# Expert weights in eight larger loads, landed in buffers of later work, with their splits spread over steps 5 to 12

## The chip, the cores and the metric

The kernel runs on one core of a Trainium2 chip. The metric is the device time of one execution in microseconds (us). The engines are TensorE (PE, with its weight loads as PEld), VectorE (DVE), ScalarE (ACT), GpSimd (POOL) and SyncE (SP), which issues all plain DMAs of this kernel; the indirect DMAs are issued by POOL.

## The reference

Attention with eight heads over eight batches: 512 local queries look at a window of 32 keys to either side and at 32 global keys, 32 global queries look at everything. Its output, 576 rows of 512 per batch, goes through a layer in which the 128 rows of highest gate score get an expert's output added.

```
s_l  = concat(scale * q_l @ k_g.T, where(|i-j| <= 32, scale * q_l @ k_l.T, -1e9))
out_l = softmax(s_l) @ concat(v_g, v_l);  out_g = softmax(scale * q_g @ k_all.T) @ v_all
x = concat(out_g, out_l) as [B, 576, 512]
scores = x @ w_gate
top = argpartition(-scores[b], 128)[:128]
out[b, top] = x[b, top] + sigmoid(scores[b, top]) * (relu(x[b, top] @ w1) @ w2)
```

## The kernel before

The attention of one batch is six pieces of work, in the order `ORDER`: local tiles L0 and L1 (128 queries, all heads), the two global halves G0 and G1, then L2 and L3. With eight batches there are 48 steps; step `i` of the loop is piece `i % 6` of batch `i // 6`. The program order on each engine is written out by hand and pipelined: in step `i` PE runs the attend matmuls of piece `i-1` (L260 for a local, L349 for a global piece), the scores of piece `i+1` (L201, L314) and the transposes of piece `i` (L238, L341). ACT then copies the transposed probabilities to SBUF (`pt`, L247 or L244) and takes the exponential of piece `i+1` (L228, L328). DVE divides the output (`x`, L280), takes the maxima (`mxl`, L215; `mx`, L318) and the gate score of each output tile (L297, with the gate row `wgb`). Each engine executes its own list in order, so whatever waits holds all that is behind it.

The expert's weights are `w1` and `w2`, 2 MiB each in fp32. Each of 16 blocks of 128x512 is split into a high part (a cast on ACT, L153) and the rest (a subtraction on POOL, L154). `load_w` loads one block of 256 KB into `ws`, a ring of three buffers (`wst`), and `split` makes the two parts. The main loop issues two loads in each of the steps 1 to 8 and, at the end of a step from step 2 on, splits all blocks loaded so far but the last. The split stands in ACT's list behind the exponential of that step, so ACT's next copy `pt` is behind it.

A batch's K, Q and V come through `load(b)` (for batch 1 issued in step 1) and `load_v(b, t)`, V in a ring of four buffers of 1040 KB. `load_rest` brings the gate row, the index constants and the masks of the ranking in step 0. Stores of finished tiles are issued by `run_stores` at the head of a step, ahead of that step's loads. `load_xg` reads a batch's global rows back from the output.

A batch's ranking is a generator, `chain`, started in step 6b+7. For batch 0 the score rows are spread in step 9 (`spread`), ranked in steps 9, 10 and 11 (`rank`, pairs of DVE instructions L395 and L397), the one-hot matrix is made in step 11 (L407), the rows are gathered in step 12 (an indirect DMA of POOL, L427, into `xe`), and the expert's work on them begins in step 14 with `expand` (transposes L448), which fills `xTh` and `xTl`; `ffn1_row`, `ffn1_turn` and `ffn1_pair` fill `hTh` and `hTl`. Which step gets how much of that work is set by `GROUPS`, `DUE` and `run_fill` in steps, not in time. L106 to L125 are the loads of the start, L287 the stores of `x`, L365 those of the global rows, L369 `load_xg`.

## Time and profile before

| what | value |
|---|---|
| time, median of 3 runs | 361.35 us (360.27 to 363.27) |
| profiled execution, its own time | 363.92 us |
| its span in the trace | 361.9 us |
| PE busy / PEld busy | 283.1 us (78%) / 224.4 us (62%) |
| DVE, ACT, POOL busy | 203.7 us (56%), 166.9 us (46%), 37.7 us (10%) |
| bytes moved by DMA | 75.89 MB, mean 210 GB/s |
| share of "DMA ws<-in_w_dram" in the chain that ended last | 9% |

The shares are means over a start that waits for loads, a long middle and an end of expert work alone. Each stretch is read by itself, by what its engines wait for.

### The profile page before, as it was taken

The numbers are of one execution on the slowest core, as the hardware profiler recorded it, in microseconds if no ns is written. First come the engines' busy times: TensorE is split into PE (matmuls) and PEld (weight loads), VectorE is DVE, ScalarE is ACT, GpSimd is POOL, SyncE is SP. The second block draws the span as 40 slices with busy tenths as digits, with TensorE's granted clock in tenths as the row PEclk, the third lists the DMA queues.
The fourth block names the chain that finished last, engine by engine and source line by source line (L and its number), as shares of the span: only waits on it lengthen the run. The fifth ranks groups of instructions, "written<-read, shape, count | busy, mean of one in ns | idle before, by whom it ended". The sixth has DMA issues, their size and how long they took to land.

```text
span 361.9 us, 14027 instructions
## 1 busy us (share of the span) xinstructions
PE 283.1 (78%) x6200; PEld 224.4 (62%) x6200; DVE 203.7 (56%) x561; ACT 166.9 (46%) x483; POOL 37.7 (10%) x38
## 2 busy tenths in 40 slices
PE   5373855367759869978787799998768999599994
PEld 2342743246537746755566788876648887389882
DVE  1142363329844748695776665787756656639122
ACT  1253755257644745673476336354763361032020
POOL 1002444141100000100200001101000011110211
PEclk9699696869989989998999999999999999779998
DMA  7996579944992696189569912995691011100100
GB/s 215 405 412 243 183 265 378 372 137 146 362 369 75 239 415 264 42 307 423 215 210 345 361 38 66 385 361 200 211 340 57 34 43 60 59 29 2 58 29 29
DMA packets 22652, 75.89 MB, mean 210 GB/s; under 512 B 4672, under 2 KB 7616, under 8 KB 17600
## 3 DMA queue, kind: packets, MB, share of 16 engines
q1 hardware_dynamic: 21312, 70.81, 52.7%
q0 software_dynamic: 1280, 4.20, 3.4%
q8 instruction: 48, 0.79, 0.9%
q14 instruction: 12, 0.10, 0.1%
HBM read 63.98 MB, written 11.01 MB: 207 GB/s over the span
## 4 chain that ended last, share of the span: by engine, by line
PE 41%; issue 17%; DMA 17%; ACT 11%; DVE 7%; SPq 3%; POOL 3%; POOLq 0%; ACTq 0%
DMA ws<-in_w_dram 9%; ACT p_t L228 5%; PE m_ps L509 5%; PE s_ps L260 5%; PE s_ps L201 5%; PE s_ps L238 5%; PE m_ps L525 4%; DMA wgb<-in_wg_dram 4%; DMA xe<-out_dram,ix 4%; PE s_ps L314 3%; ACT pt L247 3%; PE s_ps L349 3%; PE s_ps L341 2%; PE s_ps L509 2%; ACT pt L244 2%
## 5 line engine op out<-in xcount | busy, mean ns | idle before, releaser
L228 ACT ACTIVATE p_t<-s_ps,nb 128x128 f32<-128x128 f32 x256 | 69.7, 384 | 1.0
L247 ACT COPY pt<-s_ps 128x512 f32<-128x512 f32 x64 | 34.4, 589 | 61.3 <-PE s_ps L238 61.3
L260 PE MATMUL s_ps<-v_t,pt 128*32 128x65 f32 x2048 | 39.5, 229 | 27.0 <-ACT pt L247 22.5
L260 PEld LDWEIGHTS s_ps<-v_t,pt 128*32 128x32 f32 x2048 | 33.4, 115 | 36.0 <-ACT pt L247 27.8
L215 DVE TENSOR_REDUCE mxl<-s_ps 128x8 f32<-128x1024 f32 x32 | 39.0, 1220 | 29.3 <-PE s_ps L201 29.3
L201 PE MATMUL s_ps<-k_t,q_t 64*32 64x128 f32 x2048 | 40.5, 286 | 10.1 <-DMA k_t<-in_kT_dram 6.4
L238 PE MATMUL s_ps<-cs,p_t 128*128 128x128 f32 x256 | 37.3, 291 | 4.8 <-issue 2.7
L201 PEld LDWEIGHTS s_ps<-k_t,q_t 64*32 64x32 f32 x2048 | 30.7, 110 | 13.9 <-issue 11.5
L238 PEld LDWEIGHTS s_ps<-cs,p_t 128*128 128x128 f32 x256 | 29.5, 148 | 11.2 <-issue 5.5
L349 PE MATMUL s_ps<-v_t,pt 128*32 128x65 f32 x768 | 16.1, 239 | 17.2 <-ACT pt L244 17.2
L244 ACT COPY pt<-s_ps 128x768 f32<-128x768 f32 x16 | 12.8, 799 | 30.9 <-PE s_ps L341 30.9
L349 PEld LDWEIGHTS s_ps<-v_t,pt 128*32 128x32 f32 x768 | 13.3, 121 | 21.4 <-ACT pt L244 19.5
L274 DVE TENSOR_SCALAR den<-s_ps 128x8 f32<-128x8 f32 x32 | 5.2, 164 | 37.3 <-PE s_ps L260 36.0
L427 POOL DMA_INDIRECT xe<-out_dram,ix x8 | 7.9, 985 | 169.3 <-DVE junk L395 133.7
L395 DVE SCALAR_TENSOR_TENSOR junk<-r,sc,side_w 128x128 bf16<-128x128 f32 (+4 forms) x40 | 24.4, 611 | 0.9 <-ACT r L383 0.2
L297 DVE CUSTOM_DVE_ANT_0 junk<-x,wgb 128x512 bf16<-128x512 f32 x32 | 23.3, 728 | 0.3 <-DMA wgb<-in_wg_dram 0.2
L280 DVE TENSOR_TENSOR x<-s_ps,rec 128x512 f32<-128x512 f32 x32 | 22.1, 691 | 1.2 <-DVE rec L276 0.2
L509 PE MATMUL m_ps<-xTh,w1h 128*128 128x256 f32 x76 | 19.8, 291 | 2.8 <-DVE hTl L512 2.8
L397 DVE SCALAR_TENSOR_TENSOR junk<-r,sc,side_w 128x544 bf16<-128x544 f32 (+4 forms) x40 | 20.6, 516 | 2.1 <-ACT nb L222 0.2
L314 PE MATMUL s_ps<-k_t,qg_t 64*32 64x512 f32 (+1 forms) x256 | 20.1, 429 | 0.0
L509 PE MATMUL m_ps<-xTh,w1l 128*128 128x256 f32 x76 | 19.0, 283 | 0.0
L532 POOL DMA_INDIRECT out_dram<-xe,ix x8 | 8.1, 1011 | 87.8 <-DVE xe L530 63.3
(111 smaller groups left out, 474.9 us busy)
## 6 DMA issues: line engine op xcount, KB each, us to landing
v_t<-in_vw_dram SPq DMA_DIRECT2D x32, 1040.0 KB
k_t<-in_kT_dram SPq DMA_DIRECT2D x7, 1664.0 KB
out_dram<-x SPq DMA_DIRECT2D x32, 256.0 KB
q_t<-in_qT_dram SPq DMA_DIRECT2D x15, 512.0 KB
ws<-in_w_dram SPq DMA_DIRECT2D x16, 256.0 KB
k_t<-in_kT_dram SPq DMA_DIRECT2D x1, 1152.0 KB
q_t<-in_qT_dram SPq DMA_DIRECT2D x2, 256.0 KB
k_t<-in_kT_dram SPq DMA_DIRECT2D x1, 512.0 KB
```

The lines of the kernel that those rows point to most:

```text
L201: nc.tensor.matmul(out=s_ps[32 * j:32 * j + 32, hp, P * pr:P * pr + P], lhsT=q_t[t // 2][rows, pr, 32 * (c % 8):32 * (c % 8) + 32], rhs=wi ...
L215: nc.vector.tensor_reduce(out=mx, in_=s_ps.rearrange("p a (r k) -> p (a r) k", k=P), axis=AX.X, op=ALU.max)
L228: nc.scalar.activation(out=p_t[:, hp, cc], in_=s_ps[:, hp, cc], func=AF.Exp, scale=0.125, bias=nb[:, k:k + 1])
L238: nc.tensor.transpose(s_ps[:, hp, cc], p_t[:, hp, cc], ident)
L247: nc.scalar.copy(out=pt[:, hp], in_=s_ps[:, hp])
L260: nc.tensor.matmul(out=s_ps[32 * j:32 * j + 32, hp, VD * pr:VD * pr + VD], lhsT=pt[:, hp, x0:x0 + 32], rhs=v_t[:, j, NPAIR * hp + pr, :], ...
L280: nc.vector.tensor_tensor(out=xt[b, t].rearrange("p r a d -> p a r d"), in0=o_ps[:, :, :, 0:D], in1=rec.broadcast_to([P, 2, NPAIR, D]), op ...
L297: nc.vector.tensor_tensor_reduce(out=junk[:n, 0:DM], in0=xf, in1=wgb[:n], op0=ALU.mult, op1=ALU.add, scale=1.0, scalar=0.0, accum_out=dst,)
L314: nc.tensor.matmul(out=o_, lhsT=qg_t[rows, pr, :], rhs=r_, start=True, stop=True)
L349: nc.tensor.matmul(out=og[32 * h:32 * h + 32, :], lhsT=ptg[:, P * i + 32 * h:P * i + 32 * h + 32], rhs=vts[b, c // 4][:, c % 4, NPAIR * (h ...
L395: nc.vector.scalar_tensor_tensor(out=junk[:n, 0:hi], in0=r[:n, 0:hi], scalar=s, in1=side_w[:n, P + SL - lo:P + SL - lo + hi], op0=ALU.is_g ...
L509: nc.tensor.matmul(out=h_ps, lhsT=a[:, kc, ms], rhs=xT[x_][:, kc, :], start=(i == 0), stop=(i == len(prods) - 1))
```

## The change

The eight loads of `load_w` are now pieces of different sizes. Pieces 0 and 1 are 1 MiB of `w1` each and land in tiles named `hTh` and `hTl`, pieces 2 to 5 are 256 KB blocks of `w2` in the four `xe` buffers, pieces 6 and 7 are 512 KB of `w2` in `xTh` and `xTl`. These buffers are used by the expert's work only from step 12 on. `LOADW` says in which step each piece is issued, `SPLITS` how many of the 16 blocks are split in which step. The ring `ws` shrinks to two buffers. The gate row moves from `load_rest` into `load(0)`; all four V tiles of batch 0 are issued ahead of the loop; `load_rest` moves to step 1 behind `load(1)`; in every step the stores and `load_xg` come behind the loads.

```
-RESTL, LATE, WFIRST = 0, 4, 1
+RESTL, LATE = 1, 4
+LOADW = {2: (0,), 3: (1,), 6: (2, 3), 7: (4, 5), 8: (6, 7)}
+SPLITS = {5: 1, 6: 2, 7: 2, 8: 4, 9: 2, 10: 1, 11: 2, 12: 2}
...
-    wst = ctx.enter_context(tc.tile_pool(name="wst", bufs=3))
+    wst = ctx.enter_context(tc.tile_pool(name="wst", bufs=2))
...
             load_v(0, 0)
+            nc.sync.dma_start(out=wgb, in_=wg)
             nc.sync.dma_start(out=q_t[0][:, :, P:], in_=qT[b, 0, :, :, P:])
...
+    def load_w(k):
+        if k < 2:
+            s = moe.tile([P, 2, FF], FP32, name=("hTh", "hTl")[k])
+            nc.sync.dma_start(out=s, in_=w1[:, 2 * k:2 * k + 2])
+            for n in range(4):
+                raw[4 * k + n] = s[:, n // 2, 512 * (n % 2):512 * (n % 2) + 512]
+        elif k < 6:
+            s = moe.tile([P, DM], FP32, name="xe", bufs=4)
+            nc.sync.dma_start(out=s, in_=w2[:, k - 2])
+            raw[6 + k] = s
+        else:
+            s = moe.tile([P, 2, DM], FP32, name=("xTh", "xTl")[k - 6])
+            m = 2 * k - 8
+            nc.sync.dma_start(out=s, in_=w2[:, m:m + 2])
+            raw[8 + m], raw[9 + m] = s[:, 0], s[:, 1]
...
     load(0)
-    load_v(0, 1)
-    wl = []
+    for t in range(1, NT):
+        load_v(0, t)
+    wl = list(range(2 * KC + MC))
...
         if i < nstep:
-            run_stores()
-            if s == 0:
+            if s == 0 and b > 0:
                 load_v(b, 2)
-            if i == RESTL:
-                load_rest()
             if s == 1:
-                load_v(b, 3)
+                if b > 0:
+                    load_v(b, 3)
                 if b + 1 < B:
                     load(b + 1)
             if s == 5:
-                load_xg(b)
                 if b + 1 < B:
                     load_v(b + 1, 0)
                     load_v(b + 1, 1)
-            if WFIRST <= i < WFIRST + 8:
-                wl.append(load_w(2 * (i - WFIRST)))
-                wl.append(load_w(2 * (i - WFIRST) + 1))
+                load_xg(b)
+            if i == RESTL:
+                load_rest()
+            for k in LOADW.get(i, ()):
+                load_w(k)
+            run_stores()
...
-        if i > WFIRST:
-            while wl[-2:-1] if WFIRST <= i < WFIRST + 8 else wl:
-                split(*wl.pop(0))
+        for _ in range(SPLITS.get(i, 0)):
+            split(wl.pop(0))
```

Three places in the order of the instructions follow. The first is ACT's list in steps 1 to 4 of the kernel before. L247 and L244 are the copies `pt` of a local and a global piece, L328 and L228 exponentials, L153 the casts of the splits.

```order
8 L247 COPY pt<-s_ps 128x512 x2
9 L328 ACTIVATE pg<-s_ps,nbg 128x64
10 L328 ACTIVATE pg<-s_ps,nbg 128x5x96
11 L244 COPY pt<-s_ps 128x768
12 L328 ACTIVATE pg<-s_ps,nbg 128x64
13 L328 ACTIVATE pg<-s_ps,nbg 128x5x96
14 L153 CAST w1h<-ws 128x512 x3
15 L244 COPY pt<-s_ps 128x768
16 L222 ACTIVATE nb<-mxl 128x8
17 L228 ACTIVATE p_t<-s_ps,nb 128x128 x8
18 L153 CAST w1h<-ws 128x512 x2
```

In the change the same stretch of ACT's list has no cast (all its line numbers behind `load_w` are 17 higher).

```order
8 L264 COPY pt<-s_ps 128x512 x2
9 L345 ACTIVATE pg<-s_ps,nbg 128x64
10 L345 ACTIVATE pg<-s_ps,nbg 128x5x96
11 L261 COPY pt<-s_ps 128x768
12 L345 ACTIVATE pg<-s_ps,nbg 128x64
13 L345 ACTIVATE pg<-s_ps,nbg 128x5x96
14 L261 COPY pt<-s_ps 128x768
15 L239 ACTIVATE nb<-mxl 128x8
16 L245 ACTIVATE p_t<-s_ps,nb 128x128 x8
```

The three casts that stood between an exponential and the copy of step 3 are gone from there. The second place is ACT's list in steps 8 and 9 of the change, where most casts stand now (L400 and L403 copy the score rows that `spread` turned).

```order
34 L345 ACTIVATE pg<-s_ps,nbg 128x64
35 L345 ACTIVATE pg<-s_ps,nbg 128x5x96
36 L180 CAST w1h<-hTl 128x512 x3
37 L180 CAST w2h<-xe 128x512
38 L400 COPY r<-m_ps 128x512
39 L403 COPY r<-m_ps 128x32
40 L261 COPY pt<-s_ps 128x768
41 L239 ACTIVATE nb<-mxl 128x8
42 L245 ACTIVATE p_t<-s_ps,nb 128x128 x8
43 L180 CAST w2h<-xe 128x512 x2
44 L264 COPY pt<-s_ps 128x512 x2
```

Before, two casts stood at the first of these two places and one at the second; the block at the first place grew to four, and from here on two, one, two and two casts stand at the end of the steps 9 to 12. The third place is SP's list behind the first loads. Before:

```order
10 L125 DMA v_t<-in_vw_dram 128x2080 x2
11 L632 DMA wgb<-in_wg_dram 128x512
12 L633 DMA cs<-in_const_dram 128x133
13 L634 DMA side_w<-in_edge_dram 128x128
14 L635 DMA side_w<-in_edge_dram 128x128
15 L125 DMA v_t<-in_vw_dram 128x2080
16 L115 DMA q_t<-in_qT_dram 128x1024
17 L116 DMA k_t<-in_kT_dram 128x3328
18 L117 DMA q_t<-in_qT_dram 128x1024
19 L118 DMA qg_t<-in_qgT_dram 128x128
20 L160 DMA ws<-in_w_dram 128x512 x2
21 L287 DMA out_dram<-x_317 128x512
```

In the change, the same loads and what follows them:

```order
12 L118 DMA q_t<-in_qT_dram 128x1024
13 L119 DMA k_t<-in_kT_dram 128x3328
14 L120 DMA q_t<-in_qT_dram 128x1024
15 L121 DMA qg_t<-in_qgT_dram 128x128
16 L649 DMA cs<-in_const_dram 128x133
17 L650 DMA side_w<-in_edge_dram 128x128
18 L651 DMA side_w<-in_edge_dram 128x128
19 L160 DMA hTh<-in_w_dram 128x2048
20 L304 DMA out_dram<-x_313 128x512
21 L160 DMA hTl<-in_w_dram 128x2048
22 L304 DMA out_dram<-x_380 128x512
```

The weights still stand behind all loads of batches 0 and 1, but as two transfers of 1 MiB that wait for no buffer.

## Rows read from the trace of the kernel before

**Rows 1.** The waits of the whole span: who waited for whom, us in total, times, longest.

```profile
ACT w2h L153 <- DMA ws<-in_w_dram: 14.2, 3, 8.5
ACT w1h L153 <- DMA ws<-in_w_dram: 6.8, 3, 4.8
PE s_ps L201 <- DMA k_t<-in_kT_dram: 6.4, 1, 6.4
```

**Rows 2.** The timeline, ACT's part: start, duration, engine, line, operation, count, and in brackets the idle time before it and what ended it. Two copies `pt` without a split ahead of them, then the three longest waits of casts.

```profile
22.93 1.07 ACT L247 COPY pt<-s_ps 128x512 f32<-128x512 f32 x2 [1.18 <-PE s_ps L238]
27.13 0.80 ACT L244 COPY pt<-s_ps 128x768 f32<-128x768 f32 x1 [2.36 <-PE s_ps L341]
...
33.49 1.27 ACT L153 CAST w1h<-ws 128x512 fp32r<-128x512 f32 x2 [4.79 <-DMA ws<-in_w_dram]
...
55.89 0.62 ACT L153 CAST w2h<-ws 128x512 fp32r<-128x512 f32 x1 [5.33 <-DMA ws<-in_w_dram]
...
73.85 0.62 ACT L153 CAST w2h<-ws 128x512 fp32r<-128x512 f32 x1 [8.53 <-DMA ws<-in_w_dram]
```

**Rows 3.** The timeline, PE's part: the attend matmuls that open steps 1, 2, 3, 4, 7, 9, 10, 11, 12 and 13 (L260 local, L349 global), and the transposes of step 3 (L341).

```profile
19.48 1.14 PE L260 MATMUL s_ps<-v_t,pt 128*32 128x65 f32 x64 [1.16 <-ACT pt L247]
...
24.05 1.13 PE L260 MATMUL s_ps<-v_t,pt 128*32 128x65 f32 x64 [1.16 <-ACT pt L247]
...
27.98 0.89 PE L349 MATMUL s_ps<-v_t,pt 128*32 128x65 f32 x48 [0.72 <-ACT pt L244]
...
29.89 0.88 PE L341 MATMUL s_ps<-cs,pg 128*128 128x128 f32 x6
...
36.76 1.53 PE L349 MATMUL s_ps<-v_t,pt 128*32 128x65 f32 x48 [5.78 <-ACT pt L244]
...
57.53 1.96 PE L260 MATMUL s_ps<-v_t,pt 128*32 128x65 f32 x64 [6.34 <-ACT pt L247]
...
75.22 1.53 PE L349 MATMUL s_ps<-v_t,pt 128*32 128x65 f32 x48 [7.91 <-ACT pt L244]
...
81.49 0.89 PE L349 MATMUL s_ps<-v_t,pt 128*32 128x65 f32 x48 [0.72 <-ACT pt L244]
...
86.06 1.14 PE L260 MATMUL s_ps<-v_t,pt 128*32 128x65 f32 x64 [0.94 <-ACT pt L247]
...
90.64 1.15 PE L260 MATMUL s_ps<-v_t,pt 128*32 128x65 f32 x64 [0.94 <-ACT pt L247]
...
96.47 1.17 PE L260 MATMUL s_ps<-v_t,pt 128*32 128x65 f32 x64 [0.98 <-ACT pt L247]
```

**Rows 4.** SP's timeline: two pairs of the weight loads with the time that SP spent at them.

```profile
25.94 9.86 SPq L160 DMA_DIRECT2D ws<-in_w_dram  x2
...
66.70 9.47 SPq L163 DMA_DIRECT2D ws<-in_w_dram  x2
```

**Rows 5.** Stretches of the span: from:to, length, busy us (and instructions) of PE, PEld, DVE, ACT, POOL, then the granted TensorE clock as a share of full speed, the DMA engines' busy share, and GB/s.

```profile
0.00:8.50 8.50, 5.22 (x76) 2.15 (x76) 0.88 (x3) 1.49 (x2) 1.19 (x6) 1.00 0.70 211
8.50:19.50 11.00, 3.69 (x76) 3.10 (x76) 1.90 (x2) 3.53 (x12) 0.00 (x0) 0.69 1.03 399
19.50:28.70 9.20, 7.19 (x224) 5.11 (x224) 5.00 (x14) 5.62 (x16) 0.00 (x0) 1.00 1.03 408
28.70:35.90 7.20, 2.28 (x85) 1.70 (x73) 1.83 (x4) 1.75 (x4) 1.71 (x2) 0.94 0.59 223
...
51.20:57.50 6.30, 0.00 (x0) 0.00 (x0) 1.26 (x3) 1.61 (x4) 1.62 (x2) 0.84 1.02 360
57.50:67.30 9.80, 8.60 (x176) 5.79 (x176) 5.31 (x14) 5.74 (x16) 4.11 (x4) 0.75 1.00 380
...
75.20:98.80 23.60, 18.38 (x607) 14.63 (x607) 17.10 (x46) 16.11 (x50) 5.50 (x5) 0.91 0.60 209
98.80:288.00 189.20, 161.59 (x4011) 128.40 (x4012) 126.30 (x353) 100.33 (x295) 6.83 (x7) 0.97 0.64 238
```

**Rows 6.** A DMA issue of the page's part 6: what it moves, times, size.

```profile
wgb<-in_wg_dram SPq DMA_DIRECT2D x1, 256.0 KB
```

**Rows 7.** DVE beside POOL: POOL's subtraction of one split and a ranking instruction of DVE of 128x256 that began 0.32 us after it; then the same instruction a batch later, with no work on POOL.

```profile
84.34 1.27 POOL L154 TENSOR_TENSOR w2l<-ws,w2h 128x512 fp32r<-128x512 f32 x1 [5.32 <-ACT w2h L153]
84.66 1.23 DVE L395 SCALAR_TENSOR_TENSOR junk<-r,sc,side_w 128x256 bf16<-128x256 f32 x1
...
118.75 0.48 DVE L395 SCALAR_TENSOR_TENSOR junk<-r,sc,side_w 128x256 bf16<-128x256 f32 x1
```

**Rows 8.** The line L297 (gate scores), its 32 instructions on `x`: min/median/max duration in ns, first and last start.

```profile
L297 DVE CUSTOM_DVE_ANT_0 junk<-x,wgb x32: 679/682/1219, 22.9 to 307.0; 128x512 bf16<-128x512 f32 x32
```

**Rows 9.** DVE's timeline at the turn from step 11 to step 12: the one-hot matrix, then the maxima that the next exponential needs.

```profile
93.17 0.82 DVE L407 TENSOR_TENSOR oh<-slot,rank 128x640 f16<-128x640 f16 x1
...
94.95 1.22 DVE L215 TENSOR_REDUCE mxl<-s_ps 128x8 f32<-128x1024 f32 x1
```

**Rows 10.** The timeline at the first gather: the exponential of step 12 on ACT, the gather on POOL, and the PE work that waits for it.

```profile
96.56 2.18 ACT L228 ACTIVATE p_t<-s_ps,nb 128x128 f32<-128x128 f32 x8
...
97.13 1.12 POOL L427 DMA_INDIRECT xe<-out_dram,ix  x1 [11.52 <-DVE ix L425]
...
106.65 1.08 PE L448 MATMUL m_ps<-cs,xe 128*128 128x128 f32 x4 [2.61 <-DMA xe<-out_dram,ix]
```

**Rows 11.** The last line of the view of the tile `xe`: the time from issue to landing of its DMAs.

```profile
DMA to landing us min/median/max: 2.7/3.3/9.5
```

More of the change, by code (lines that the diff above doesn't have):

```diff
@@ L150, with split @@
     slot16 = cst.tile([P, NST * P], FP16, name="slot16")
-    def split(hi, lo, src):
+    raw = {}
+    def load_w(k):
[13 more added lines that the diff above has]
+            raw[8 + m], raw[9 + m] = s[:, 0], s[:, 1]
+    def split(k):
+        if k < 2 * KC:
+            c = (slice(None), k // 2, slice(512 * (k % 2), 512 * (k % 2) + 512))
+            hi, lo = w1h[c], w1l[c]
+        else:
+            hi, lo = w2h[:, k - 2 * KC], w2l[:, k - 2 * KC]
+        src = raw.pop(k)
         nc.scalar.copy(out=hi, in_=src)
         nc.gpsimd.tensor_tensor(out=lo, in0=src, in1=hi.bitcast(FP32), op=ALU.subtract)
-    def load_w(k):
-        s = wst.tile([P, 512], FP32, name="ws")
-        if k < 2 * KC:
-            kc, f = k // 2, slice(512 * (k % 2), 512 * (k % 2) + 512)
-            nc.sync.dma_start(out=s, in_=w1[:, kc, f])
-            return w1h[:, kc, f], w1l[:, kc, f], s
-        k -= 2 * KC
-        nc.sync.dma_start(out=s, in_=w2[:, k])
-        return w2h[:, k], w2l[:, k], s
     xt = {}
@@ L631, in load_rest @@
     def load_rest():
-        nc.sync.dma_start(out=wgb, in_=wg)
         nc.sync.dma_start(out=cs[:, P:o], in_=const[:, P:o])
```

## The prediction

> **What bounds the kernel now.** I read the waits of the whole span first. ACT's casts of the weight splits wait 14.2 + 6.8 = 21.0 us for `ws` to land, in six waits [rows 1]. The timeline shows where: the three long ones of 4.79, 5.33 and 8.53 us end at 33.5, 55.9 and 73.9 us [rows 2]. Behind each stands a copy `pt`, and PE's attend matmuls, next in PE's list, sit idle for 5.78, 6.34 and 7.91 us [rows 3]. So up to 76 us an engine that is not loaded stops the whole pipeline. Then why the data are late: SP spends 9.86 and 9.47 us at pairs of weight loads [rows 4], because a ring of three buffers lets the next load go only when the split of an earlier block has freed one; the split waits for the load and the load for the split. In the stretch 28.7 to 35.9 us the DMA queues move only 223 GB/s, while they move 399 and 408 in the two stretches ahead, where SP is not held [rows 5]. Elsewhere PE waits for a load only once, 6.4 us for the rest of K of batch 0 [rows 1]. From 98.8 to 288 us the queues move 238 GB/s at a DMA share of 0.64 [rows 5]: no bound there.
>
> **What the steps cost without the stalls.** I count from the attend of step 1 (19.48) to that of step 13 (96.47): 76.99 us for twelve steps [rows 3]. The same steps undisturbed:
> - local to local: 4.58 (86.06 to 90.64); five such gaps, steps 1, 5, 6, 7 and 11: 22.9. Step 12, in which the ranking ends, takes 5.83 (90.64 to 96.47).
> - local to G0, steps 2 and 8: 27.98 - 24.05 = 3.93 each, 7.86.
> - G0 to G1 in step 3: transposes end at 29.89 + 0.88 = 30.77, the copy takes 0.80 [rows 2], so some 3.7 after 27.98. In step 9 the score rows are spread as well; before it took 6.27 (75.22 to 81.49), with attends at half clock (1.53 against 0.89 us). Between 3.7 and 6.27 I take 5.2.
> - G1 to L2, steps 4 and 10: 86.06 - 81.49 = 4.57 each, 9.14.
>
> Sum: 22.9 + 5.83 + 7.86 + 3.7 + 5.2 + 9.14 = 54.6, that is **22.4 us less**. It is more than the 21.0 of waits because PE comes back from each stall at a lower clock: in 57.5 to 67.3 us the granted clock is 0.75 [rows 5], and an attend takes 1.96 instead of 1.14 us [rows 3].
>
> **Do the new loads come in time?** The queue works through its bytes at about 0.405 MB/us when SP is not held [rows 5]. By the order of SP's list and the shapes in it, 9.7 MB stand ahead of and including K of batch 1, 10.4 MB through the masks, 12.8 MB through `hTl`. At 28.7 us the kernel before had moved 9.9 MB (8.5 us at 211 GB/s, 11.0 at 399 and 9.2 at 408 [rows 5]); so `hTh` lands near 32 and `hTl` near 36 us. The first split from `hTh` stands at the end of step 5, near 44 us by the steps above, the first from `hTl` in step 7, near 52. Step 7 issues V3 of batch 1, then the loads of batch 2, then two `w2` blocks: 4.4 MB from about 43 us on, 11 us, so they land near 55, and `xTh`, `xTl` near 59. They are split in steps 9 to 12, from 62 us on; batch 2's scores start near 66. Nothing is closer than 6 us. V of batch 1 is free to load once G1 of batch 0 has used its buffers, near 33, lands near 40, and is needed at 46. The buffers lent cost nothing: the first write of the expert's own work to them is in step 14, behind POOL's last subtraction.
>
> **What the change costs.**
> - The gate row stands ahead of the rest of K, for which PE waits [rows 1]: 0.262 MB [rows 6] at 0.4 MB/us, **0.65 us**.
> - Sixteen casts of 0.62 [rows 2] stay. ACT idles 1.18 us ahead of a local copy and 2.36 ahead of a global one while PE transposes [rows 2], which hides one or three of them. Two casts (1.24) in steps 6, 9, 11 and 12 stick out by less than 0.1 each, four in step 8 by nothing against the spread that follows: **0.4 us** in all, for the copies of the score rows too.
> - POOL against DVE. A ranking instruction took 1.23 us beside a subtraction and 0.48 without one [rows 7], 0.75 more; a gate score at most 1219 ns against 682 [rows 8], 0.54 more. Seven subtractions now stand in steps 9 to 12 and the last of step 8's four reach into step 9, and there DVE is full: the one-hot matrix ends at 93.99 and only then come the output and the maxima at 94.95 on which the next exponential waits [rows 9]. The bounds are nothing (DVE free at the time) and 11 x 0.65 = 7.2. I take three collisions on the path, two of the rankings and the one-hot matrix: **1.8 us**.
> - The gather of batch 0 stands on POOL behind the two subtractions of step 12. Before, step 12's exponential ended at 96.56 + 2.18 = 98.74 [rows 10]; a cast of 0.62 and two subtractions of 1.27 [rows 7] behind it end at 101.9, where the gather went at 97.13: 4.8 us later by the clock of the steps. It landed 9.5 us after issue, most gathers after 3.3 [rows 10, 11]; it shared the queues with batch 3's loads, which now are issued some 3 us sooner. PE waited 2.61 us for it. Between 2.6 us better and 4.8 worse I take **nothing**.
> - Stores and `load_xg` behind the loads: a batch's loads are 3.9 MB, 10 us of queue. Each store is of a tile not written again for most of a batch (some 27 us), the gather that reads it comes six steps later, and `xg` is read two steps later. Nothing, and up to 1 us where `xg` is late for DVE.
>
> Sum: 22.4 - 0.65 - 0.4 - 1.8 = **19.5 us**. The span of 361.9 becomes 342.4, the profiled execution's own 363.92 becomes 344.4, and the median of the runs, 2.57 below that execution, 361.35 - 19.5 = **342 us**.
>
> **The rivals.**
> - *POOL holds DVE for whole instructions.* The row shows a DVE instruction with two SBUF inputs beside POOL's subtraction ending 0.28 us after it, as if it had begun only near the end [rows 7]. If each of the 11 subtractions of steps 8 to 12 catches one at its start, the cost is 11 x 1.27 = 14.0 instead of 1.8: 354 us. The row speaks for the mechanism; against the size, DVE often waits for PE in these steps, and the maxima and outputs read PSUM. With the late gather, 347 to 355. [...]
> - *The loads come late, and it is slower.* Everything hangs on the pace of the queue between 36 us and the first scores of batch 2 near 66: 8 MB. At 0.405 they take 20 us. At 209 GB/s, the pace of 75.2 to 98.8 us [rows 5], they take 38, and PE waits 8 us: 350. The gain is gone when K of batch 2 lands 20 us late, below 8/50 = 0.16 MB/us; at 0.14 it would be 369. Against it: no stretch of the rows is that slow, and the slow ones are those in which SP had nothing it could issue.
> - *It doesn't do what it says.* If the middle of the kernel ran at a pace that the start doesn't set, the time won would be lost again by 288 us: 361. Against it: expert work is dealt out by steps, and DMA has a third to spare there [rows 5].
> - *Better than the sum*: no collisions on the path and the gather free of its wait, 342 - 1.8 - 2.6 = 337.6 or less.
>
> **How the numbers follow.** My forecast (337 to 347) has 0.69, the first rival (347 to 355) 0.13, better than 337 0.06, no change 0.05, slower 0.07. The time predicted is 342. A range of 336 to 351 leaves out about 2 in 10: slower, no change, the dear end of the first rival and the far end of the good case. A measurement of this kernel tells about 1% from no change, 357.7 to 365: faster 0.88, same 0.05, slower 0.07.
>
> **What would show it.** Right: no wait of a cast for a DMA, attends of steps 4, 7 and 9 near 32, 46 and 55 us, step 13 near 77, PE's first K wait 0.65 us longer, and the rows from 98.8 us on found again some 19 us sooner. Wrong: casts in steps 8 to 12 waiting for `xe` or `xTh`; PE waiting for K or V of batch 1 or 2; rankings of over 1.2 us in steps 9 to 11 with maxima behind them; a wait for the first gather of over 5 us.

## The result

| | before | change |
|---|---|---|
| median of 4 runs each, same chip | 361.93 us (360.27 to 363.27) | 350.50 us (348.81 to 352.80) |
| ratio, 95% interval | | 0.9691 [0.9615, 0.9766] |
| profiled execution, its own time | 363.92 us | 348.81 us |
| its span | 361.9 us | 346.8 us |
| PE busy | 283.1 us (78%) | 280.8 us (81%) |
| the unaltered change again, second chip | 364.51 us | 354.57 us, 0.9746 [0.9692, 0.9799] |
| the same, third chip | 363.50 us | 353.73 us, 0.9745 [0.9689, 0.9802] |

The medians are over all runs of a kernel; the ratios, here and below, compare only the fast runs, which lie within 1.5% of the fastest run of the same kernel. The change is faster by 11.4 us here and by 9.9 and 9.8 us on the two other chips, where the forecast said 19.5. The two profiled executions lie 15.1 us apart, because the one of before is longer than its median and the one of the change is the fastest of its four. So the ledger of the traces explains 15.1 us, and a second profile of the change, of 353.27 us (the run `control` below), is read beside it.

The line numbers of the changed kernel are 17 higher (L260 is L277 and so on). PE's waits in it, those that a DMA ended or that the profile can put down to nothing ("issue"): engine, line, what it waited for, us in total, times, longest.

```profile
PE s_ps L277 <- issue: 8.2, 6, 2.0
...
PE s_ps L218 <- DMA k_t<-in_kT_dram: 5.6, 1, 5.6
...
PE s_ps L331 <- issue: 2.8, 2, 1.4
PE s_ps L218 <- issue: 2.8, 4, 1.1
...
PE s_ps L255 <- issue: 2.2, 1, 2.2
PE s_ps L366 <- issue: 2.1, 3, 1.5
...
PE m_ps L465 <- DMA xe<-out_dram,ix: 1.3, 2, 1.0
```

The list of ACT's waits holds no DMA any more; the 21.0 us of [rows 1] are gone, and no cast waits for a load. What is new is the sum of PE's "issue" waits, 8.2 + 2.8 + 2.8 + 2.2 + 2.1 = 18.1 us. In the same view of the kernel before they are 10.7:

```profile
PE s_ps L260 <- issue: 4.4, 3, 2.0
...
PE s_ps L201 <- issue: 3.6, 3, 1.4
...
PE s_ps L238 <- issue: 2.7, 1, 2.7
```

PE's timeline of the change answers to [rows 3]: the attends of steps 1, 2 and 3, then all of PE's work from the attend of step 4 to the gap in step 6, then some later attends and, last, the scores and the transposes of step 13 (L277 local, L366 global, L218 and L331 scores, L255 transposes, L199 the mask).

```profile
20.04 1.96 PE L277 MATMUL s_ps<-v_t,pt 128*32 128x65 f32 x64 [1.16 <-ACT pt L264]
...
25.85 1.14 PE L277 MATMUL s_ps<-v_t,pt 128*32 128x65 f32 x64 [1.16 <-ACT pt L264]
...
29.79 0.89 PE L366 MATMUL s_ps<-v_t,pt 128*32 128x65 f32 x48 [0.73 <-ACT pt L261]
...
33.51 0.65 PE L366 MATMUL s_ps<-v_t,pt 128*32 128x65 f32 x31 [0.72 <-ACT pt L261]
35.63 0.47 PE L366 MATMUL s_ps<-v_t,pt 128*32 128x65 f32 x17 [1.46 <-issue]
36.03 1.16 PE L218 MATMUL s_ps<-k_t,q_t 64*32 64x128 f32 x64
37.12 1.09 PE L255 MATMUL s_ps<-cs,p_t 128*128 128x128 f32 x8
38.05 0.38 PE L199 MATMUL s_ps<-cb 128*128 128x256 bf16 x2
39.37 1.14 PE L277 MATMUL s_ps<-v_t,pt 128*32 128x65 f32 x64 [0.94 <-ACT pt L264]
40.44 1.16 PE L218 MATMUL s_ps<-k_t,q_t 64*32 64x128 f32 x64
41.68 1.09 PE L255 MATMUL s_ps<-cs,p_t 128*128 128x128 f32 x8
42.61 0.38 PE L199 MATMUL s_ps<-cb 128*128 128x256 bf16 x2
43.94 0.59 PE L277 MATMUL s_ps<-v_t,pt 128*32 128x65 f32 x25 [0.94 <-ACT pt L264]
46.49 0.82 PE L277 MATMUL s_ps<-v_t,pt 128*32 128x65 f32 x39 [1.96 <-issue]
47.24 1.96 PE L218 MATMUL s_ps<-k_t,q_t 64*32 64x128 f32 x64
49.13 1.75 PE L255 MATMUL s_ps<-cs,p_t 128*128 128x128 f32 x8
52.04 1.14 PE L277 MATMUL s_ps<-v_t,pt 128*32 128x65 f32 x64 [1.16 <-ACT pt L264]
...
58.49 0.36 PE L277 MATMUL s_ps<-v_t,pt 128*32 128x65 f32 x9 [0.87 <-issue]
...
61.65 0.89 PE L366 MATMUL s_ps<-v_t,pt 128*32 128x65 f32 x48 [0.72 <-ACT pt L261]
...
81.80 1.13 PE L277 MATMUL s_ps<-v_t,pt 128*32 128x65 f32 x64
...
85.39 0.25 PE L331 MATMUL s_ps<-k_t,qg_t 64*32 64x32 f32 x4 [1.42 <-issue]
86.12 1.09 PE L255 MATMUL s_ps<-cs,p_t 128*128 128x128 f32 x8 [0.48 <-ACT p_t L245]
```

The reader sees that no attend waits over 1.16 us for `pt`, where three waited 5.78 to 7.91 before. But PE now stops in the middle of an attend, with all its data there: after 31 of 48 matmuls in step 4 and after 25 of 64 in step 6. Between these two gaps stand 17 + 64 + 8 + 2 + 64 + 64 + 8 + 2 + 25 = 254 matmuls, with as many weight loads 508 instructions. The queues of the change, by kind: packets, MB, share of 16 engines:

```profile
q1 hardware_dynamic: 20160, 70.81, 54.5%
...
q8 instruction: 48, 0.79, 0.9%
```

0.79 MB in 48 packets is 16 KB a packet, and PE's 6200 matmuls and 6200 loads divided by 48 are 258 instructions. So I take q8, the queue of the kind "instruction", to bring PE's program, some 258 instructions a packet by this count, and the 508 between the two gaps are two packets of 254. The trace's single DMA records give the time of each packet. All 13 gaps of PE over 0.55 us end 1.3 to 1.6 us after the end of such a packet, and so do all seven of the kernel before. The gaps up to step 13, and two packets without one (times from the start of the span, as in the views):

| packet of the change, us | DMA share in the 3 us before it | PE's gap ends at, length |
|---|---|---|
| 33.25 to 34.31 | 1.03 | 35.63, 1.46 |
| 44.13 to 45.04 | 0.99 | 46.49, 1.96 |
| 56.12 to 57.12 | 1.08 | 58.49, 0.87 |
| 62.37 to 63.37 | 1.05 | 64.68, 0.60 |
| 76.42 to 77.42 | 0.98 | 78.76, 0.83 |
| 82.97 to 84.04 | 1.07 | 85.39, 1.42 |
| 69.37 to 70.33 | 0.01 | none |
| 90.05 to 90.94 | 0.99 | none |

Of all 48 packets 25 followed 3 us at a share of 0.95 or more, and 13 of them ended a gap; of the other 23 none did. Which of the 25 stop PE is a matter of the time left. The places of the gaps lie some 127 matmuls or a multiple of it apart, so the places that the other packets serve can be counted; what follows is an estimate from that count, for packets 2 to 41. A packet starts in the median 0.7 us after PE has passed the place before its own where the share was 0.5 or less (12 packets), and 3.9 us after it where the share was 0.95 or more (24). PE stops where it reaches the packet's place less than about 1.3 us after the packet's end.

The stretches that hold the first two gaps, the one behind the second, and the long rest, in the columns of [rows 5]:

```profile
33.50:35.60 2.10, 0.65 (x31) 0.49 (x31) 0.00 (x0) 2.07 (x9) 0.00 (x0) 1.00 0.99 405
...
43.90:46.50 2.60, 0.60 (x28) 0.49 (x28) 0.00 (x0) 2.57 (x10) 0.00 (x0) 1.00 1.02 388
46.50:52.00 5.50, 4.38 (x111) 3.62 (x110) 2.89 (x6) 1.29 (x4) 1.27 (x1) 0.69 1.01 371
...
94.60:273.00 178.40, 154.39 (x3847) 122.13 (x3846) 121.55 (x339) 95.89 (x287) 7.59 (x7) 0.99 0.62 229
```

In both gaps the DMA engines are full (0.99 and 1.02). After the second the granted clock is 0.69 (0.50 from 47.2 to 50.4 us), and the scores take 1.96 instead of 1.16 us. The long rest moves 229 GB/s at a share of 0.62, about as before.

### The profile page after: what moved, and what is told of

Its sections match the earlier page's. It is cut to its first block, busy times and chain, and to the rows that moved or that the text cites. A ratio compares the mean times of both kernels' runs of the same rounds, so it can differ in the third digit from the quotient of the medians.

```text
span 346.8 us, 14013 instructions
## 1 busy us (share of the span) xinstructions
PE 280.8 (81%) x6200; PEld 219.7 (63%) x6200; DVE 207.7 (60%) x561; ACT 166.2 (48%) x483; POOL 40.5 (12%) x38
## 2 busy tenths in 40 slices
DMA packets 21501, 75.89 MB, mean 219 GB/s; under 512 B 4545, under 2 KB 7489, under 8 KB 16193
## 3 DMA queue, kind: packets, MB, share of 16 engines
q1 hardware_dynamic: 20160, 70.81, 54.5%
## 4 chain that ended last, share of the span: by engine, by line
PE 52%; issue 19%; ACT 12%; DMA 7%; DVE 6%; POOL 1%; SPq 1%; POOLq 0%; ACTq 0%; DVEq 0%
PE s_ps L218 8%; PE s_ps L255 8%; PE s_ps L277 6%; PE m_ps L526 6%; ACT p_t L245 5%; PE m_ps L542 5%; ACT pt L264 5%; PE s_ps L366 4%; PE s_ps L331 3%; PE s_ps L358 3%; DMA k_t<-in_kT_dram 3%; DMA out_dram<-x 2%; PE s_ps L526 2%; DMA xe<-out_dram,ix 2%; ACT pt L261 2%
## 5 line engine op out<-in xcount | busy, mean ns | idle before, releaser
L277 PE MATMUL s_ps<-v_t,pt 128*32 128x65 f32 x2048 | 40.3, 230 | 24.5 <-ACT pt L264 16.3
L277 PEld LDWEIGHTS s_ps<-v_t,pt 128*32 128x32 f32 x2048 | 33.7, 115 | 34.0 <-ACT pt L264 21.5
L218 PE MATMUL s_ps<-k_t,q_t 64*32 64x128 f32 x2048 | 42.4, 292 | 8.5 <-DMA k_t<-in_kT_dram 5.6
L218 PEld LDWEIGHTS s_ps<-k_t,q_t 64*32 64x32 f32 x2048 | 31.5, 112 | 13.5 <-issue 11.1
L255 PE MATMUL s_ps<-cs,p_t 128*128 128x128 f32 x256 | 36.8, 289 | 3.8 <-issue 2.2
L255 PEld LDWEIGHTS s_ps<-cs,p_t 128*128 128x128 f32 x256 | 29.0, 147 | 10.1 <-issue 5.5
L444 POOL DMA_INDIRECT xe<-out_dram,ix x8 | 8.6, 1080 | 149.7 <-DVE junk L412 90.8
L414 DVE SCALAR_TENSOR_TENSOR junk<-r,sc,side_w 128x544 bf16<-128x544 f32 (+4 forms) x40 | 22.3, 557 | 2.1 <-ACT pt L261 0.2
L297 DVE TENSOR_TENSOR x<-s_ps,rec 128x512 f32<-128x512 f32 x32 | 22.1, 691 | 1.2 <-DVE rec L293 0.2
L331 PE MATMUL s_ps<-k_t,qg_t 64*32 64x512 f32 (+1 forms) x256 | 20.4, 416 | 2.8 <-issue 2.8
L366 PE MATMUL s_ps<-v_t,pt 128*32 128x65 f32 x768 | 15.2, 222 | 7.3 <-ACT pt L261 5.0
L366 PEld LDWEIGHTS s_ps<-v_t,pt 128*32 128x32 f32 x768 | 12.0, 110 | 11.8 <-ACT pt L261 7.3
```

What stands on the lines that cost most here:

```text
L218: nc.tensor.matmul(out=s_ps[32 * j:32 * j + 32, hp, P * pr:P * pr + P], lhsT=q_t[t // 2][rows, pr, 32 * (c % 8):32 * (c % 8) + 32], rhs=wi ...
L255: nc.tensor.transpose(s_ps[:, hp, cc], p_t[:, hp, cc], ident)
L277: nc.tensor.matmul(out=s_ps[32 * j:32 * j + 32, hp, VD * pr:VD * pr + VD], lhsT=pt[:, hp, x0:x0 + 32], rhs=v_t[:, j, NPAIR * hp + pr, :], ...
L331: nc.tensor.matmul(out=o_, lhsT=qg_t[rows, pr, :], rhs=r_, start=True, stop=True)
L366: nc.tensor.matmul(out=og[32 * h:32 * h + 32, :], lhsT=ptg[:, P * i + 32 * h:P * i + 32 * h + 32], rhs=vts[b, c // 4][:, c % 4, NPAIR * (h ...
L414: nc.vector.scalar_tensor_tensor(out=junk[:n, lo:ST], in0=r[:n, lo:ST], scalar=s, in1=side_w[:n, 0:ST - lo], op0=ALU.is_gt, op1=ALU.mult, ...
```

## The experiments

Theory A: the missing gain is PE's own instruction packets, late behind full load queues, and the clock after such a gap; before, the long stalls covered them. Theory B: it is the subtractions on POOL that hold DVE in steps 9 to 12. Theory C: it is PE's lower clock after a wait (in the change 0.50 from 13 to 20 us, behind the wait for K), alone. Twelve kernels ran. Each ratio is to the kernel before on the same chip.

### Which of the theories

`change_again` is the change, unaltered, as the base on this chip.

> The changed kernel once more, unaltered, on the chip of the next three kernels, as their base line. Expected: 350 us, ratio to the kernel before 0.965 to 0.975; PE's idle time that ends with nothing but its own issue about 18 us in total.

354.57 us, 0.9746 [0.9692, 0.9799]; PE's issue waits are 18.0 us. The gaps are no accident of one profile.

`small_rows` breaks the long rows of K and V into shorter ones at the same bytes:

```
-        k_t = ld.tile([P, NPAIR, KW], FP32, name="k_t")
+        k_t = ld.tile([P, NPAIR, KW + 8], FP32, name="k_t")[:, :, 0:KW]
...
+        v_ = vld.tile([P, 4, H * VD + 8], FP32, name="v_t")
+        vts[b, t] = v_[:, :, 0:H * VD].rearrange("p j (h d) -> p j h d", d=VD)
```

> The changed kernel with rows of K and V padded in SBUF, so that each row of a transfer is 3328 or 2080 bytes instead of 13312 or 8320; bytes, transfers and order as they were. Theory A (PE's gaps are its own instructions, 16 KB packets that come through the same DMA engines as the data and arrive late behind large rows): PE's issue gaps fall from 18 us to under 9, 3 to 6 us faster than the changed kernel. Theory B (the loss is POOL's lock on DVE) and theory C (the loss is the half clock after a stall alone): gaps as they were, within 1 us of the changed kernel.

356.69 us, 0.9811 [0.9757, 0.9864], with issue waits of 21.4 us. The load queue now has 35136 packets instead of 20160, and nothing is gained; the run is 2.1 us slower than `change_again`, and its step 1 begins at 23.04 us instead of 20.46. That the packet waits behind long single rows is refuted for these lengths.

`no_sub`:

```
+    nc.gpsimd.memset(w1l.bitcast(FP32), 0.0)
+    nc.gpsimd.memset(w2l.bitcast(FP32), 0.0)
...
-        nc.gpsimd.tensor_tensor(out=lo, in0=src, in1=hi.bitcast(FP32), op=ALU.subtract)
```

> The changed kernel without the 16 subtractions on POOL; the low parts of the weights are zeros written once at the start, so the expert's result is less exact. Theory B: ranking instructions beside no POOL work take 0.5 to 0.8 us again and the one-hot matrix 0.82 instead of 1.82; 2 us faster than the changed kernel or more. Theory A: the DVE rows change as said, but PE's issue gaps stay near 18 us, and the time falls by 2 us at most.

351.49 us, 0.9626 [0.9557, 0.9695]: 3.1 us below `change_again`, more than the 2 us of theory B, with intervals that just touch. The one-hot matrix takes 0.82 us again, and the gather's wait falls to 0.2; the issue waits stay, at 15.9. But the steps 12 and 13, behind the rankings and the one-hot matrix, take 12.35 us together, against 12.16 in `change_again`: with DVE free, gaps of 1.36 and 0.69 us and an attend of 1.51 us instead of 1.14 hold PE there. Step 14, in which PE waits for the gather, takes 3.93 instead of 6.46; 1.3 of the difference is that wait; what the other 1.2 is, is not shown. So what gain can be placed lies where the gather no longer stands behind subtractions, not where DVE is free of them.

`v_once`:

```
     def load_v(b, t):
+        if b > 0:
+            vts[b, t] = vts[0, t]
+            return
```

> The changed kernel without the V loads of batches 1 to 7, which use V of batch 0: 28 loads of 1040 KB left out, 29 of 76 MB. Theory A: the queues are full for less of the time, PE's issue gaps fall from 18 us to under 8, and the time falls by 5 to 10 us. Theories B and C: no load is waited for after the first K, so the time stays within 2 us of the changed kernel.

348.11 us, 0.9573 [0.9521, 0.9624]: 6.5 us below `change_again`, with issue waits of 8.5 instead of 18.0 us at 46.06 MB instead of 75.89. PE's program is the same. Its timeline, the attends of steps 4, 6 and 7 (all line numbers 3 higher than in the change):

```profile
34.37 0.65 PE L369 MATMUL s_ps<-v_t,pt 128*32 128x65 f32 x31 [0.72 <-ACT pt L264]
36.72 0.47 PE L369 MATMUL s_ps<-v_t,pt 128*32 128x65 f32 x17 [1.70 <-issue]
...
45.04 1.15 PE L280 MATMUL s_ps<-v_t,pt 128*32 128x65 f32 x64 [0.94 <-ACT pt L267]
...
49.62 0.48 PE L280 MATMUL s_ps<-v_t,pt 128*32 128x65 f32 x17 [1.16 <-ACT pt L267]
51.69 1.26 PE L280 MATMUL s_ps<-v_t,pt 128*32 128x65 f32 x47 [1.59 <-issue]
```

The gap in step 4 is at the same 31 matmuls as in the change, where the queues are still as full (1.03 ahead of its packet). The one in step 6 is gone. Its packet comes at 42.32 to 43.19 in the records, well before PE reaches the place near 45.6, and in the 3 us ahead of the packet the DMA share of `v_once` is 0.29:

```profile
39.30:42.30 3.00, 2.06 (x121) 1.74 (x127) 0.95 (x6) 2.93 (x10) 0.00 (x0) 1.00 0.29 74
```

So the gaps have fixed places in PE's program, and they open where the queues are full. That carries theory A's place and condition. Its size is another matter: of the 6.2 us between the spans (344.5 against 350.7) only 2.2 lie in steps 1 to 12, which take 60.5 instead of 62.7. The run takes V's rows and V's buffers away together, so it doesn't say which part of the traffic delays the packet.

### Edits that might win something back

`early_splits` splits sooner:

```
+LOADW = {1: (0,), 2: (1,), 4: (2, 3), 6: (4, 5), 7: (6, 7)}
+SPLITS = {2: 3, 3: 2, 4: 2, 5: 2, 6: 2, 7: 2, 8: 2, 9: 1}
```

> The changed kernel with its eight pieces and lent buffers, but splits in steps 2 to 9 as before (three in step 2, then two a step) and the pieces issued one to two steps sooner to match. If the landing buffers alone made the gain, the time stays near the changed kernel (ratio to before 0.97). If it is the distance between a load and its split, ACT's casts wait for DMA again, near 3 us in step 2 and some 5 us more for the w2 blocks split in the step in which they are issued, and the ratio is 0.98 to 0.995.

354.99 us, 0.9812 [0.9719, 0.9906]. ACT's timeline has the two waits that came back:

```profile
34.57 1.66 ACT L180 CAST w1h<-hTh 128x512 fp32r<-128x512 f32 x3 [5.30 <-DMA hTh<-in_w_dram]
...
67.63 0.62 ACT L180 CAST w2h<-xTh 128x512 fp32r<-128x512 f32 x1 [6.41 <-DMA xTh<-in_w_dram]
```

The steps that hold them take 8.42 and 9.00 us. This is the stall of the kernel before, made again by the tables alone: what the change lives on in steps 1 to 12 is that a cast stands behind the landing of its block. They take 71.0 us here, between the 77.0 of before and the 61.8 of the change. The whole time shows little of it, and its interval overlaps those of the change, because steps 13 to 15 take 16.8 us against 19.3 in the change: no subtraction stands ahead of the first gather, and PE's waits for gathers sum to 0.3.

`stores_first` moves `run_stores` and `load_xg` back to the head of the step:

```
+            run_stores()
+            if s == 5:
+                load_xg(b)
             if s == 0 and b > 0:
...
-                load_xg(b)
...
-            run_stores()
```

> The changed kernel with the stores and the read-back of the global rows ahead of a step's loads again. Prediction's view: the order costs and gives nothing, within 1% of the changed kernel (ratio to before 0.965 to 0.98). Rival: SP held by a store's wait keeps the queue emptier, so PE's issue gaps fall below 14 us and it is 2 to 4 us faster.

353.94 us, 0.9778 [0.9695, 0.9860], against 0.9691, 0.9746 and 0.9745 for the change: no gain, and a loss that its interval doesn't separate. The rival's sign isn't there either: the issue waits are 16.3 us, not below 14.

`warm_start` fills PE's wait for K with matmuls that nobody reads:

```
+        if i == 0:
+            w_ps = m_tile()
+            for _ in range(20):
+                nc.tensor.matmul(out=w_ps, lhsT=wz[:, 0:P], rhs=wz, start=True, stop=True)
```

> The changed kernel with 20 matmuls on zeros in PE's wait for the rest of the first K (9.4 to 15.0 us). Theory C (part of the loss is the half clock after the wait): the scores of step 0 take 1.2 instead of 2.0 us, the attend of step 1 1.1 instead of 2.0, step 2 begins 2 to 3 us sooner, and the ratio falls by 0.005 to 0.01 against the changed kernel. Theory A and B: the steps from 2 on keep their lengths.

352.46 us, 0.9649 [0.9540, 0.9757]; its six runs lie far apart, from 347.06 to 356.66. In the profile the scores behind the wait take 1.79 us, not the 1.2 of theory C. Step 1 takes 4.58 us, as undisturbed, with an attend of 1.14 us, where the first profile of the change has 5.81 and 1.96; step 2 begins 1.2 us sooner. But `early_splits` and `stores_first`, which don't touch the start, have 4.57 and 4.56 too. So the length of step 1 differs between executions with the same start, and the edit is not shown to have cured it.

`splits_by_9` brings the splits to an end in step 9, with the loads sooner:

```
+LOADW = {2: (0,), 3: (1,), 4: (2, 3, 4, 5), 5: (6, 7)}
+SPLITS = {4: 2, 5: 2, 6: 2, 7: 4, 8: 4, 9: 2}
```

> The changed kernel with all w2 pieces issued in steps 4 and 5, ahead of batch 1's V, and all splits done in steps 4 to 9 (2, 2, 2, 4, 4, 2). Theory B: no subtraction is left beside the rankings of steps 10 and 11 and the one-hot matrix (0.82 instead of 1.82 us), step 12 is 1.5 to 2 us shorter, the first gather is no longer held by subtractions: 2 to 4 us faster, ratio 0.962 to 0.969. Theory A: PE's gaps stay 14 to 20 us in total, at other places, and can eat 2 us of it or give as much.

349.98 us, 0.9646 [0.9565, 0.9726]. The ratio lies where theory B put it, but its interval overlaps those of the change, which did not run on this chip. The one-hot matrix takes 0.82 us again, but the rankings of steps 9 and 10 still collide (1.51 and 1.55 us), and the issue waits are 15.7. Step 12 is not shorter (5.91 us against 5.59), step 13 is, by 0.8.

### A base, the cause, and the sum of the edits

`control` is the unaltered change.

> The changed kernel unaltered, as the base line of the next three on their chip: ratio to the kernel before 0.965 to 0.978.

353.73 us, 0.9745 [0.9689, 0.9802]; profiled execution 353.27 us. Its gaps up to step 12 are one more and mostly longer than in the first profile: 1.69, 1.68, 1.34, 1.87, 1.15 and 1.71 us, at 31 of 48 matmuls in step 4 and 25 of 64 in step 6 again.

`more_loads` adds 72 loads of 256 KB that nobody needs, in the middle of the kernel:

```
+    dump = cst.tile([P, 512], FP32, name="dump")
...
+            if 20 <= i < 42 and 2 <= s <= 4:
+                for n in range(6):
+                    d_ = dump if n % 3 == 0 else wst.tile([P, 512], FP32, name="ws")
+                    nc.sync.dma_start(out=d_, in_=w2[:, n])
```

> The changed kernel with 72 further loads of 256 KB (18.9 MB) into buffers that nothing reads, six a step in 12 steps between 20 and 40 in which the queues are near idle. Theory A (PE stops for its own instructions where the queues are full): up to the 20th step as the changed kernel, behind it some 4 to 8 new issue gaps of 0.6 to 2.5 us, PE's issue waits at 22 us or more against 16 to 18, and 5 to 10 us slower. Rival (the gaps only happen to fall in full stretches): no new gaps, within 2 us of the changed kernel.

391.00 us, 1.0766 [1.0691, 1.0842], 37 us above `control`. The issue waits are 13.3 us, fewer than in `control`, where theory A's forecast had 22 or more: that forecast failed. But the run answers another question than the one that I put. PE's longest wait in sum:

```profile
PE s_ps L278 <- DMA v_t<-in_vw_dram: 44.3, 4, 14.4
```

Most of the loss is PE waiting for V, because the extra loads go through a ring of two buffers and one of their own, and SP stood at them with V's loads behind it:

```profile
SPq L686 <- DMA ws<-in_w_dram: 33.6, 34, 8.4
SPq L686 <- DMA dump<-in_w_dram: 33.1, 14, 7.3
```

So theory A has no clean test by added traffic. One of this run's gaps, of 0.82 us, followed a DMA share of 0.92.

`ring_kept` is the kernel before with the new order of loads alone, its ring of three and its splits kept:

```
-RESTL, LATE, WFIRST = 0, 4, 1
+RESTL, LATE, WFIRST = 1, 4, 1
...
             load_v(0, 0)
+            nc.sync.dma_start(out=wgb, in_=wg)
...
-        nc.sync.dma_start(out=wgb, in_=wg)
...
-    load_v(0, 1)
+    for t in range(1, NT):
+        load_v(0, t)
...
-            run_stores()
...
+            run_stores()
```

> The kernel before with only the order of the loads changed: gate row ahead of the rest of K, V of batch 0 ahead of the loads of batch 1, stores and read-back behind a step's loads; the ring of three buffers and the splits as they were. Expected: ACT's casts wait for DMA some 20 us again, ratio to before 0.99 to 1.01; the gain is in the pieces and the spread splits.

364.36 us, 0.9963 [0.9911, 1.0015]. ACT's waits for the weights are as before:

```profile
ACT w2h L154 <- DMA ws<-in_w_dram: 16.5, 2, 11.6
ACT w1h L154 <- DMA ws<-in_w_dram: 6.2, 3, 3.3
```

The order of the loads alone is worth nothing that can be measured; the gain is in the buffers and the places of the splits, of which `early_splits` takes away the places.

`three_edits` is the change with the edits of `warm_start` and `splits_by_9`, and the gate row behind the rest of K:

```
-            nc.sync.dma_start(out=wgb, in_=wg)
             nc.sync.dma_start(out=q_t[0][:, :, P:], in_=qT[b, 0, :, :, P:])
             nc.sync.dma_start(out=k_t[:, :, 2 * P:KW], in_=kT[b, :, :, 2 * P:KW])
+            nc.sync.dma_start(out=wgb, in_=wg)
```

> The changed kernel with three edits: 20 matmuls on zeros in PE's first wait, all splits done in steps 4 to 9, and the gate row behind the rest of K. If the three add up (1 to 2, 2 to 4, 0.6 us), ratio 0.952 to 0.963 and 4 to 6 us faster than the control; if gaps and half clock eat them, 0.965.

352.55 us, 0.9708 [0.9656, 0.9760], 1.2 us below `control` with intervals that overlap; its issue waits are 17.3 us. PE's timeline, the attend of step 1:

```profile
18.07 1.01 PE L277 MATMUL s_ps<-v_t,pt 128*32 128x65 f32 x53 [1.16 <-ACT pt L264]
20.82 0.65 PE L277 MATMUL s_ps<-v_t,pt 128*32 128x65 f32 x11 [1.75 <-issue]
```

This is theory A in one place. Step 1 begins 2.0 us sooner than in the first profile of the change, and after 53 of 64 matmuls PE stops for its packet. That came from 18.40 to 19.50 us, where the change's came from 18.54 to 19.64 and stopped nobody: PE reached the place 2 us sooner, the packet came 0.1 us sooner. Step 2 begins at 26.01 instead of 25.85. The edits don't add up, and none is shown to beat the change.

## Why the prediction was right, and where its size came from

The direction and the mechanism held: casts that wait for blocks in a small ring were the stall, and the time came out of steps 1 to 12. The size was too large by 8 to 10 us on the medians. That the range of 336 to 351 held is luck: 350.5 is half a microsecond inside it, and by the ratios on the other two chips the change would be at 352.7. The time lies where the first rival was put (347 to 355), but the runs don't show its mechanism, POOL holding DVE, to be what cost the rest. The steps of the two traces, attend to attend, against the forecast:

| | forecast | before | change | `control` |
|---|---|---|---|---|
| step 1 | 4.58 | 4.57 | 5.81 | 6.19 |
| step 2 | 3.93 | 3.93 | 3.94 | 3.94 |
| step 3 | 3.7 | 8.78 | 3.72 | 3.73 |
| step 4 | 4.57 | 6.44 | 5.86 | 6.09 |
| step 5 | 4.58 | 4.58 | 4.57 | 4.57 |
| step 6 | 4.58 | 9.75 | 8.10 | 6.32 |
| step 7 | 4.58 | 6.57 | 4.57 | 5.92 |
| step 8 | 3.93 | 11.12 | 5.04 | 6.05 |
| step 9 | 5.2 | 6.27 | 5.42 | 5.97 |
| steps 10, 11 | 9.15 | 9.15 | 9.14 | 9.14 |
| step 12 | 5.83 | 5.83 | 5.59 | 6.46 |
| steps 1 to 12 | 54.6 | 76.99 | 61.76 | 64.38 |

**The step that failed** is the term "22.4 us less". Its mechanism was right and its size was not: 15.2 in the first trace, 12.6 in `control`. I took the lengths of undisturbed steps as what remains when the stalls go. The step of 4.58 us that I took as the measure (86.06 to 90.64 of before) is one whose instruction packet, 84.06 to 85.41, came with the DMA engines nearly idle (0.03) in the 3 us ahead of it. Steps 4 to 9 of the change (33.50 to 67.07 us) run at a DMA share of 0.92. Packets stop PE there for 1.46, 1.96, 0.87 and 0.60 us, in steps 4, 6, 8 and 9, and these steps are 1.3, 3.5, 1.1 and 0.2 us longer than forecast: 6.1 of the missing 7.2. Steps 4 and 9 are longer by less than their gaps (1.3 of 1.46 us, 0.2 of 0.60), step 6 by more than its own (3.5 of 1.96), with the clock at 0.69 behind it. Step 1 is 1.2 us longer, at a granted clock of 0.50 from 20 to 23 us, where before has 1.00; all three profiles of the unaltered change have this length (5.81, 6.14 and 6.19 us), the kernel before, `early_splits` and `stores_first` have not. In `control` the steps 4, 6, 7, 8, 9 and 12, each with a gap, make 8.1 of the missing 9.8, and step 1 makes 1.6.

The forecast had one such gap in it unseen: the 5.83 us of step 12, which I put down to the ranking, hold a gap of 1.08 us of the kernel before:

```profile
93.44 0.85 PE L201 MATMUL s_ps<-k_t,q_t 64*32 64x128 f32 x37 [1.08 <-issue]
```

It is the only one before in the twelve steps. The packets for the places in steps 4, 7 and 9 came at 32.11 to 33.19, 51.44 to 52.39 and 68.06 to 68.99 us there, at a DMA share of 0.98 to 1.03 too, and all three lie inside the long waits of [rows 3]. In these steps (in step 7 only `control` has a gap) two delays lay side by side, and I counted the one that I saw as if it were alone. In step 6, the dearest, it was otherwise: before, that place's packet came at 44.92 to 45.80, after a share of 0.51, and PE passed the place near 48.3 without a stop; the change fills the queue there to 0.99. Shown are the gaps' fixed places in the program, a packet at the end of each, and full queues ahead of it; `v_once` has 9.5 us less of issue waits and is 6.5 us shorter. That they make up nearly the whole difference is read from the ledger.

**The terms that came as forecast.**
- The loads were in time: no cast waits, and batch 2's K and V are in no wait of PE. The late-loads rival is out for this table; `early_splits`, with the casts some steps sooner, shows what it would have looked like. The attends that I put near 32, 46, 55 and 77 us came at 33.5, 52.0, 61.7 and 81.8: the first is late by step 1, the others by the gaps ahead of them as well.
- The gate row: step 1 begins at 20.04 instead of 19.48, 0.56 us, forecast 0.65; in `change_again` and `control` it is 1.0 and 1.2. The sign that I named for it, a longer K wait, failed: the wait is 5.6 us instead of 6.4 because PE's scores ahead of it took 1.96 us instead of 1.16; the scores behind it begin 0.4 us later.
- The casts, forecast 0.4: no attend of the rows above waits longer for `pt` than the 1.16 of before.
- POOL against DVE, forecast 1.8: the collisions lie where they were put, and their price isn't shown. DVE's timeline, two rankings at the turn to step 11 and the one-hot matrix:

```profile
70.24 1.23 DVE L412 SCALAR_TENSOR_TENSOR junk<-r,sc,side_w 128x256 bf16<-128x256 f32 x1
...
71.51 1.55 DVE L414 SCALAR_TENSOR_TENSOR junk<-r,sc,side_w 128x416 bf16<-128x416 f32 x1
...
79.64 1.82 DVE L424 TENSOR_TENSOR oh<-slot,rank 128x640 f16<-128x640 f16 x1
```

Behind it stand the maxima for which ACT's next exponential waits:

```profile
83.66 0.21 ACT L239 ACTIVATE nb<-mxl 128x8 f32<-128x8 f32 x1 [1.92 <-DVE mxl L232]
```

Without POOL at work they took 0.48, 0.65 and 0.82 us ([rows 7, 9], and `no_sub` for the 128x416). Step 13 is 2.0 us longer than before (6.58 against 4.57), near the 1.8 forecast, but PE's gap of 1.42 us lies in it too: behind that gap the transposes wait only 0.48 us more for this exponential. In `control`, where the one-hot matrix took 1.83 us, they follow a gap of 1.38 without a wait and the step takes 5.99; in `no_sub`, with no subtraction at all, it takes 6.23. The two rankings cost steps 10 and 11 nothing. So DVE does lose time beside POOL, 0.75, 0.90 and 1.00 us in these three instructions where a subtraction alone takes 1.27; that it is held for whole ones is not shown. Next to nothing of it is seen on the path; the first rival's 14 us would have needed every subtraction to catch an instruction there.
- The first gather, taken as nothing between 2.6 better and 4.8 worse. POOL's timeline:

```profile
86.66 3.34 POOL L181 TENSOR_TENSOR w2l<-xTl,w2h 128x512 fp32r<-128x512 f32 x2 [4.05 <-ACT w2h L180]
90.17 1.12 POOL L444 DMA_INDIRECT xe<-out_dram,ix  x1 [0.17 <-POOL w2l L181]
```

It does stand behind the last two subtractions, and PE waits 1.0 us for its data instead of 2.6, but 2.8 in `control`. With steps 14 and 15 1.8 us shorter than before (12.70 against 14.54), steps 13 to 15 together change by 0.2.

The sum in the traces: 15.2 won in steps 1 to 12, 0.6 lost ahead of them, 0.2 lost in steps 13 to 15, 0.6 won in all the rest: 15.1, the difference of the spans. The rest gives nothing back, so the third rival is out. The last 3.7 us between 15.1 and the 11.4 of the medians are the choice of executions: in `control`'s trace 12.6 are won in steps 1 to 12, 1.2 lost ahead of them, 1.3 lost in steps 13 to 15 and 1.0 won in the rest, 11.1 in all.

**What stays open.** Why an instruction packet starts late under full queues: not for the length of the rows (`small_rows`). `more_loads` was to raise the effect and failed. What decides whether PE's clock falls with a gap (in step 6 one of 1.96 us was followed by 0.69 granted, one of 1.68 us in `control` by scores of 1.16 us) was not tried, nor why it differs in step 1 (1.00 before and 0.50 in the change, from 20 to 23 us). What a collision of POOL and DVE costs where no gap lies beside it has no run.

## What to carry to other kernels

A stall covers whatever else is late at the time, so take the length of a step without it from a stretch with the same load on the queues, not from a quiet one. PE's program of 12,400 small instructions comes here in 48 packets, and those behind full queues start late (by the estimate above 3.9 us after PE has passed the place before their own, against 0.7): look for "issue" gaps at a fixed place in its list, compare them with the instruction queue's packets (in the same time base), and count them into any plan that fills the queues more densely. A small ring of landing buffers holds not only its own loads but everything behind them on the issuing queue (SP stood 9.86 us at one pair of loads [rows 4]); where later buffers are still idle, landing there takes the wait away, as long as the first use stands well behind the landing; its price here is fuller queues, a DMA share of 0.92 in steps 4 to 9 instead of 0.76.

## What the runs showed of the hardware

The instruction queue moves 48 packets of 16 KB. Of those behind 3 us at a DMA share of 0.95 or more (25 in the change), some (13) are followed by a stop of PE in the middle of a row of matmuls, of 0.6 to 2.7 us in the two kernels' traces, and PE goes on 1.3 to 1.6 us after the packet's end. The issue waits, nearly all of them such stops, sum to 10.7 us in the kernel before, 18 to 21 us in three profiles of the change, 8.5 with 30 MB less to move. Shorter rows of the loads beside it, 35136 packets instead of 20160, did not help (21.4 us). PE's pace at the same place of the same program differs between executions: the first scores of step 0 took 1.16 us in `control` and 1.96 in the first profile of the change. A DVE instruction of 0.82 us with two SBUF inputs took 1.82 beside POOL's subtraction, and POOL's own pair of 2.49 to 2.50 us took 3.10.
